# Three one-bank PSUM tiles in place of one three-bank tile at the opening of an expert stage, and a column copied out in three parts

## The chip, the cores and the metric

The kernel runs on one core of one Trainium2 chip. The metric is the time of one execution on the device in microseconds (us). The engines are named as in the profile: PE does the matmuls (PEld its weight loads), DVE, ACT and POOL are the vector, scalar and gpsimd engines, SP issues the DMAs. PSUM is the buffer into which PE writes; it has eight banks of 512 f32 values per partition, and every one of the eight is in use in the stage that is changed.

## The reference

```python
scores = scale * np.matmul(q_pool, k.transpose(0, 1, 3, 2))   # 2 x 8 heads, q pooled by 2
x = softmax(scores) @ v                                        # -> x of 1152 tokens x 512
gate = 1.0 / (1.0 + np.exp(-(x @ w_gate)))                     # first layer, d_ff 1536
x = (gate * (x @ w_val)) @ w_out
logits = x @ w_gate2                                           # expert stage, E = 8
P = np.exp(logits - logits.max())
for _ in range(8):
    P /= P.sum(1, keepdims=True) + 1e-09
    P /= P.sum(0, keepdims=True) + 1e-09
    P *= N / E
for e in range(E):
    out += P[:, e:e + 1] * (np.maximum(x @ w1[e], 0.0) @ w2[e])
```

Three parts follow each other: attention, a gated first layer, and eight experts of 1024 hidden columns whose outputs are weighted by an eight-fold normalised routing matrix. Matmuls are made of two halves of each number (high and low part), three matmuls for one product.

## The kernel before, in words

The last thing the first layer does is its output product, one 128-column block `c` at a time, for `c` = 0 to 3. Each block is 1152 tokens wide and lies in PSUM as three thirds of `TB` = 384 tokens, each third in a bank of its own. For `c` = 3 the PSUM pools of the first layer are closed and the eight banks of the expert stage are laid out: `B0`, `B1`, `X0`, then one tile `psz` of three banks, whose banks are named `Y1`, `y0`, `y1`, then `X1` and `Y0`. The block `c` = 3 is computed in `psz`. The step `x3` (function `take_x3`) copies all three banks to SBUF with one ACT instruction of 1152 columns; the steps `d10` and `d11` read the first third and half of the second on DVE.

From there on the three banks of `psz` do different work. Each expert is computed in two halves; a half-expert is numbered `hx`, 0 to 15, and takes three phases: two first products (`first_product`, matmul lines 903 to 905) and a second product (`second_product`, lines 1318 to 1323 and the plain product on 1353 to 1355). The products follow a seven-product scheme on 2 x 2 blocks: results are added up in the bank pairs `X0 X1`, `Y0 Y1` and `B0 B1`, copied from one pair to another by the ACT steps `go` (`psB<-psX`, `psB<-psY`, `psB<-psz`), and taken out by DVE (`take`, line 1276, tile `acc`). `y0` holds the plain product of the last 128 tokens (128x512, taken by one DVE instruction of 512 columns), and in the first half-experts the gate logits (lines 1455 and 1458) and their transposes (1469); `y1` holds half of the logits and the column sums of the routing (line 1540). In half-experts with an odd `hx` the second product begins in `Y0 Y1`, in even ones in `X0 X1`.

Every instruction of this stage is a `step` with an engine, a due time, durations and the names of the banks that it reads or writes. `arrange` merges the steps into one list with a greedy rule (which engine is free first, given the planner's own durations), and each engine works through its share in that order. `SHIFT` holds offsets of the due times, by step name. The semaphores are not the planner's: the framework sets them from the reads and writes of each tile. They show in the profile as waits. In the profile `psX` is `X0` or `X1`, `psB` is `B0` or `B1`, `psY` is `Y0`, and `psz` stands for `Y1`, `y0` or `y1`, to be told apart by the line and by the columns.

Of the kernel before, what the change touches and what calls it, by code (L numbers as in the profile page):

```python
# [126 lines left out]
def moe_stack_kernel(ctx: ExitStack, tc: tile.TileContext, q, k, v, wg1, wv1, wo1, wg2, w1, w2, out):  # L127
# [789 lines left out]
    with ExitStack() as pb:  # L917
# [48 lines left out]
        for c in range(KD):  # L966
# [10 lines left out]
            if c < KD - 1:  # L977
                ps = ps_b.tile([P, 3, 512], F32, tag="b", name="pso")
            else:
                pbs.close()  # L980
                ps_f = ctx.enter_context(tc.tile_pool(name="ps_f", bufs=1, space=PSUM, reuse_waits="tile"))
                bank = {k: ps_f.tile([P, 512], F32, tag=k, name=f"ps{k[0]}") for k in ("B0", "B1", "X0")}
                ps = ps_f.tile([P, 3, 512], F32, tag="z", name="psz")
                bank.update((k, ps[:, n]) for n, k in enumerate(("Y1", "y0", "y1")))
                bank.update((k, ps_f.tile([P, 512], F32, tag=k, name=f"ps{k[0]}")) for k in ("X1", "Y0"))
            for fc in range(NFF):
                wt = w[:, :, fc * P:(fc + 1) * P]
                for n in range(3):
                    cols = slice(n * TB, (n + 1) * TB)
                    three(  # L990
                        ps[:, n, 0:TB], wt[:, 0], wt[:, 1], gs[fc][:, 0, cols], gs[fc][:, 1, cols],
                        fc == 0, fc == NFF - 1,
                    )
# [394 lines left out]
    def inputs():  # L1388
# [23 lines left out]
        def take_x3():  # L1412
            copy(xt[3].rearrange("p (n w) -> p n w", n=3), ps[:, :, 0:TB])

# [10 lines left out]
        for n, w in ((0, TB), (1, HT - TB)):  # L1425
            step(
                f"d1{n}", "DVE", t - 2, (470, 270)[n], (560, 360)[n],
                lambda n=n, w=w: join(
                    nc.vector, high(2)[:, n * TB:n * TB + w], ps[:, n, 0:w], high(2)[:, n * TB:n * TB + w],
                    ALU.subtract,  # L1430
                ), (), (), [("x", 2)], least=t, ps=("Y1", "y0")[n],
            )
        step("x3", "ACT", t - 2, 1050, 1140, take_x3, (), (), [("x", 3)], least=t, ps="Y1 y0 y1")
        split("b1", xc[1][:, 0], high, 2, t - 1, ["d10", "d11"])
        split("c1", xb[1][:, 0], high, 3, t, ["x3"])
        less("t1", t + 0.5, lambda: low(0), lambda: low(3), lambda: low(2), ["x3", "g0h", "g0l"], 0, 2, 3)
        split("g1", xc[1][:, 1], low, 0, t + 1.5, ["t1"])
        split("h1", xb[1][:, 1], low, 3, t + 2, ["x3"])
# [151 lines left out]
```

## Time and profile before

| | us |
|---|---|
| median of 3 runs | 1276.05 (1274.38 to 1276.24) |
| the profiled execution | 1273.15 |
| span of its trace | 1271.4 |
| PE busy | 1241.3 |
| DVE busy | 1071.4 |
| ACT busy | 780.0 |
| POOL busy | 710.8 |

Busy times are sums over the span. The rest of the profiled execution's time lies outside the span. The first layer's last product ends at about 516 us of the span, the expert stage takes the rest. Half-experts of the even stretch follow each other at 46 us, so a pair of them (one odd, one even) is a period of 92.32 us.

### The profile page before, as it was taken

The numbers are of one execution on the slowest core, as the hardware profiler recorded it, in microseconds if no ns is written. First come the engines' busy times: TensorE is split into PE (matmuls) and PEld (weight loads), VectorE is DVE, ScalarE is ACT, GpSimd is POOL, SyncE is SP. The second block draws the span as 40 slices with busy tenths as digits, with TensorE's granted clock in tenths as the row PEclk, the third lists the DMA queues.
The fourth block names the chain that finished last, engine by engine and source line by source line (L and its number), as shares of the span: only waits on it lengthen the run. The fifth ranks groups of instructions, "written<-read, shape, count | busy, mean of one in ns | idle before, by whom it ended". The sixth has DMA issues, their size and how long they took to land.

```text
span 1271.4 us, 23695 instructions
## 1 busy us (share of the span) xinstructions
PE 1241.3 (98%) x8924; PEld 1206.2 (95%) x8924; DVE 1071.4 (84%) x1954; ACT 780.0 (61%) x1773; POOL 710.8 (56%) x751
## 2 busy tenths in 40 slices
PE   8999999998999999999999999999999999999998
PEld 6889999998999999898999999999999999999998
DVE  7999999997666664888998898898888888888887
ACT  8999999983333322756457557556645645745753
POOL 7778888664434333653564564454555546455552
PEclk9999999999999999999999999999999999999999
DMA  5111220113222331111111111111111111111112
GB/s 163 44 48 56 58 57 13 34 35 99 83 84 85 98 100 51 48 36 34 48 52 36 51 51 34 51 51 51 48 51 37 51 51 34 51 51 51 34 34 76
DMA packets 61204, 70.50 MB, mean 55 GB/s; under 512 B 3360, under 2 KB 47776, under 8 KB 61088
## 3 DMA queue, kind: packets, MB, share of 16 engines
q1 hardware_dynamic: 61088, 68.97, 17.5%
q8 instruction: 70, 1.15, 0.4%
q14 instruction: 46, 0.38, 0.1%
HBM read 66.60 MB, written 2.36 MB: 54 GB/s over the span
## 4 chain that ended last, share of the span: by engine, by line
PE 75%; DVE 15%; ACT 5%; issue 3%; POOL 1%; DMA 1%; SPq 0%; DVEq 0%; ACTq 0%; POOLq 0%
PE psb L905 4%; PE psb L904 4%; PE psb L903 4%; PE psX L903 4%; PE psX L905 4%; PE psX L904 4%; PE psX L1318 3%; PE psX L1323 3%; PE psX L1322 3%; PE psg L542 3%; DVE pT L523 3%; PE psg L503 3%; DVE acc L1276 3%; PE psz L903 2%; PE psz L904 2%
## 5 line engine op out<-in xcount | busy, mean ns | idle before, releaser
L1058 POOL TENSOR_TENSOR sm<-xs 128x512 f32<-128x512 f32 x64 | 92.3, 1452 | 182.2 <-ACT xs L1055 155.4
L1055 ACT ACTIVATE w_two<-sm 128x512 fp32r<-128x512 f32 x128 | 77.8, 629 | 156.5 <-POOL sm L1058 134.8
L1058 POOL TENSOR_TENSOR sm<-raw_w 128x256 f32<-128x256 f32 x128 | 102.9, 824 | 125.5 <-DMA raw_w<-in_moe_w_dram 74.5
L1058 DVE TENSOR_TENSOR hb<-sm,hb 128x512 fp32r<-128x512 f32 x128 | 116.7, 934 | 24.9 <-ACT hb L1055 24.8
L542 PE MATMUL psg<-pT,vs 128*128 128x256 f32 (+1 forms) x576 | 133.0, 318 | 0.1
L1058 DVE TENSOR_TENSOR w_two<-sm,w_two 128x512 fp32r<-128x512 f32 x128 | 112.8, 890 | 5.0 <-ACT w_two L1055 5.0
L1318 PE MATMUL psX<-w_two,hb 128*128 128x256 f32 x384 | 108.7, 283 | 0.2 <-DVE acc L1274 0.2
L523 DVE TENSOR_TENSOR pT<-psg,pT 128x384 fp32r<-128x384 f32 x192 | 102.1, 552 | 7.5 <-ACT pT L519 5.5
L1323 PE MATMUL psX<-w_two,hb 128*128 128x256 f32 x384 | 108.3, 282 | 0.0
L1322 PE MATMUL psX<-w_two,hb 128*128 128x256 f32 x384 | 108.0, 281 | 0.0
L503 PE MATMUL psg<-ident,p 128*128 128x128 f32 x648 | 104.3, 273 | 0.9 <-DVE pT L523 0.3
L1055 ACT ACTIVATE hb<-sm 128x512 fp32r<-128x512 f32 x128 | 75.8, 626 | 45.6 <-POOL sm L1058 44.4
L905 PE MATMUL psb<-x,w_gv 128*128 128x384 f32 x288 | 97.0, 337 | 3.6 <-POOL w_gv L217 3.6
L904 PE MATMUL psb<-x,w_gv 128*128 128x384 f32 x288 | 96.9, 337 | 0.0
L903 PE MATMUL psb<-x,w_gv 128*128 128x384 f32 x288 | 96.9, 336 | 0.0
L542 PEld LDWEIGHTS psg<-pT,vs 128*128 128x128 f32 x576 | 91.2, 189 | 3.5 <-DVE pT L523 0.4
L519 ACT ACTIVATE pT<-psg 128x384 fp32r<-128x384 f32 x192 | 90.3, 497 | 6.0 <-PE psg L503 4.6
L1058 POOL TENSOR_TENSOR sm<-raw_w,sm 128x256 f32<-128x256 f32 x96 | 90.5, 956 | 0.3
L1058 DVE TENSOR_TENSOR w_two<-raw_w,w_two 128x512 fp32r<-128x512 f32 x96 | 75.2, 785 | 17.0 <-ACT w_two L1055 15.3
L1058 DVE TENSOR_TENSOR hb<-xs,hb 128x512 fp32r<-128x512 f32 x96 | 87.5, 924 | 0.0
L503 PEld LDWEIGHTS psg<-ident,p 128*128 128x128 f32 x648 | 78.6, 140 | 6.2 <-issue 1.2
L495 POOL TENSOR_SCALAR p<-p,sum 128x672 f32<-128x672 f32 x72 | 59.6, 828 | 38.5 <-ACT sum L491 34.8
(291 smaller groups left out, 4809.7 us busy)
## 6 DMA issues: line engine op xcount, KB each, us to landing
raw_w<-in_moe_w_dram SPq DMA_DIRECT2D x64, 512.0 KB, 3.5
raw_gv<-in_moe_w_gate_dram SPq DMA_DIRECT2D x12, 512.0 KB, 3.6
raw_gv<-in_moe_w_val_dram SPq DMA_DIRECT2D x12, 512.0 KB, 3.5
raw_o<-in_moe_w_out_dram SPq DMA_DIRECT2D x12, 512.0 KB, 3.5
vr<-in_v_dram SPq DMA_DIRECT2D x16, 288.0 KB, 2.8
kr<-in_k_dram SPq DMA_DIRECT2D x15, 288.0 KB, 2.8
qr<-in_q_dram SPq DMA_DIRECT2D x15, 256.0 KB, 3.4
out_dram<-acc SPq DMA_DIRECT2D x8, 256.0 KB, 2.2
```

The costliest lines, as they stand in the source:

```text
L503: nc.tensor.transpose(have["tpp", i, u, g][:, n * P:(n + 1) * P], have["p", i, u][:, jj * P:(jj + 1) * P], ident)
L519: nc.scalar.activation(out=p_parts(i, u, g)[0], in_=turned(i, u, g), func=AF.Copy)
L523: nc.vector.tensor_tensor(out=lo, in0=turned(i, u, g), in1=f(hi), op=ALU.subtract)
L542: nc.tensor.matmul(have["pv", i, j, n][:, 0:HALF[n][1]], have["vs", i, j][:, jj].rearrange("p a d -> p (a d)"), have["pT", i, j, n][s][:, ...
L903: nc.tensor.matmul(ps, wh, xh, start=first, stop=False, skip_group_check=more)
L904: nc.tensor.matmul(ps, wh, xl, start=False, stop=False, skip_group_check=more)
L905: return nc.tensor.matmul(ps, wl, xh, start=False, stop=last, skip_group_check=more).ins
L1055: nc.scalar.activation(out=out_, in_=in_, func=func)
L1058: eng.tensor_tensor(out=out_, in0=a, in1=b, op=op)
L1318: nc.tensor.matmul(out_, h[:, 0, cols], w[:, 0], start=(begins and kk + m == 0), stop=False, skip_group_check=True,)
L1322: nc.tensor.matmul(out_, h[:, 0, cols], w[:, 1], start=False, stop=False, skip_group_check=True)
L1323: nc.tensor.matmul(out_, h[:, 1, cols], w[:, 0], start=False, stop=(m == 1), skip_group_check=True)
```

## The change

The three-bank tile `psz` goes. `Y1`, `y0` and `y1` become tiles of one bank each, made in the same place among the others, so that each name keeps its bank. The first layer's last column block is computed in the three of them (`thirds`). The one copy `x3` becomes three, `x30` to `x32`, one for each bank, with other durations and due times for the planner and without the offset that `SHIFT` holds for the name `x3`; the steps that read the copied block depend on the parts that they need.

```diff
--- before.py
+++ after.py
@@ -976,19 +976,21 @@
             )
             if c < KD - 1:
                 ps = ps_b.tile([P, 3, 512], F32, tag="b", name="pso")
+                thirds = [ps[:, n, 0:TB] for n in range(3)]
             else:
                 pbs.close()
                 ps_f = ctx.enter_context(tc.tile_pool(name="ps_f", bufs=1, space=PSUM, reuse_waits="tile"))
-                bank = {k: ps_f.tile([P, 512], F32, tag=k, name=f"ps{k[0]}") for k in ("B0", "B1", "X0")}
-                ps = ps_f.tile([P, 3, 512], F32, tag="z", name="psz")
-                bank.update((k, ps[:, n]) for n, k in enumerate(("Y1", "y0", "y1")))
-                bank.update((k, ps_f.tile([P, 512], F32, tag=k, name=f"ps{k[0]}")) for k in ("X1", "Y0"))
+                bank = {
+                    k: ps_f.tile([P, 512], F32, tag=k, name=f"ps{k[0]}")
+                    for k in ("B0", "B1", "X0", "Y1", "y0", "y1", "X1", "Y0")
+                }
+                thirds = [bank[k][:, 0:TB] for k in ("Y1", "y0", "y1")]
             for fc in range(NFF):
                 wt = w[:, :, fc * P:(fc + 1) * P]
                 for n in range(3):
                     cols = slice(n * TB, (n + 1) * TB)
                     three(
-                        ps[:, n, 0:TB], wt[:, 0], wt[:, 1], gs[fc][:, 0, cols], gs[fc][:, 1, cols],
+                        thirds[n], wt[:, 0], wt[:, 1], gs[fc][:, 0, cols], gs[fc][:, 1, cols],
                         fc == 0, fc == NFF - 1,
                     )
             if c < KD - 1:
@@ -1409,9 +1411,6 @@
                 port=630 if eng == "DVE" else 1300,
             )
 
-        def take_x3():
-            copy(xt[3].rearrange("p (n w) -> p n w", n=3), ps[:, :, 0:TB])
-
         t = START
         split("a0", x12[:, 0], low, 0, t - 12, least=t - 12)
         less("d0", t - 14, lambda: high(0), lambda: low(1), lambda: high(0), (), 0, 1)
@@ -1426,16 +1425,21 @@
             step(
                 f"d1{n}", "DVE", t - 2, (470, 270)[n], (560, 360)[n],
                 lambda n=n, w=w: join(
-                    nc.vector, high(2)[:, n * TB:n * TB + w], ps[:, n, 0:w], high(2)[:, n * TB:n * TB + w],
+                    nc.vector, high(2)[:, n * TB:n * TB + w], thirds[n][:, 0:w], high(2)[:, n * TB:n * TB + w],
                     ALU.subtract,
                 ), (), (), [("x", 2)], least=t, ps=("Y1", "y0")[n],
             )
-        step("x3", "ACT", t - 2, 1050, 1140, take_x3, (), (), [("x", 3)], least=t, ps="Y1 y0 y1")
+        for n, k in enumerate(("Y1", "y0", "y1")):
+            step(
+                f"x3{n}", "ACT", t - 2 + 0.1 * n, 400, 490, lambda n=n: copy(xt[3][:, n * TB:(n + 1) * TB], thirds[n]),
+                (), (), [("x", 3)], least=t - 0.5 + 0.25 * n, ps=k,
+            )
+        x3 = [f"x3{n}" for n in range(3)]
         split("b1", xc[1][:, 0], high, 2, t - 1, ["d10", "d11"])
-        split("c1", xb[1][:, 0], high, 3, t, ["x3"])
-        less("t1", t + 0.5, lambda: low(0), lambda: low(3), lambda: low(2), ["x3", "g0h", "g0l"], 0, 2, 3)
+        split("c1", xb[1][:, 0], high, 3, t, x3[1:])
+        less("t1", t + 0.5, lambda: low(0), lambda: low(3), lambda: low(2), [*x3[:2], "g0h", "g0l"], 0, 2, 3)
         split("g1", xc[1][:, 1], low, 0, t + 1.5, ["t1"])
-        split("h1", xb[1][:, 1], low, 3, t + 2, ["x3"])
+        split("h1", xb[1][:, 1], low, 3, t + 2, x3[:2])
         less("f1", t + 2.5, lambda: high(3), lambda: high(3), lambda: high(2), ["c1h", "c1l", "d10", "d11"], 2, 3, eng="POOL")
         split("i1", xd[:, 1], high, 3, t + 4, ["f1"], eng="POOL")
         split("a1", x12[:, 1], low, 2, t + 5, eng="POOL")
```

In the changed kernel the profile's names are `psY` for `Y0` and `Y1` and `psy` for `y0` and `y1`, and line numbers past the change are 2 to 4 higher.

The built order of PE and POOL and that of the DMAs are the same before and after, apart from names. On ACT and DVE about a dozen instructions at the opening of the expert stage change places; after that all orders agree. These are ACT's rows at the opening, before (`xs<-psz 128x1152` is `x3`, `xc` and `xb` are operand splits, `psB<-psX` are the two `go` copies of half-expert 0, `xs<-psY` and `xs<-psz 128x288` a result taken out):

```order
656 L1055 ACTIVATE xs<-psz 128x1152
657 L1055 ACTIVATE xc_5619<-xs 128x576
658 L1055 ACTIVATE xb_4974<-xs 128x576
659 L1055 ACTIVATE psB<-psX 128x288
660 L1055 ACTIVATE xc_5619<-xs 128x576
661 L1055 ACTIVATE psB<-psX 128x288
662 L1055 ACTIVATE xs<-psY 128x288
663 L1055 ACTIVATE xb_4974<-xs 128x576
664 L1055 ACTIVATE xs<-psz 128x288
665 L1055 ACTIVATE w_two<-raw_w 128x512
```

and after:

```order
656 L1057 ACTIVATE xs<-psY 128x384
657 L1057 ACTIVATE xs<-psy 128x384 x2
658 L1057 ACTIVATE xb_4974<-xs 128x576
659 L1057 ACTIVATE xc_5621<-xs 128x576
660 L1057 ACTIVATE xb_4974<-xs 128x576
661 L1057 ACTIVATE psB<-psX 128x288
662 L1057 ACTIVATE xc_5621<-xs 128x576
663 L1057 ACTIVATE xs<-psY 128x288
664 L1057 ACTIVATE psB<-psX 128x288
665 L1057 ACTIVATE w_two<-raw_w 128x512
666 L1057 ACTIVATE xs<-psY 128x288
```

The three copies stand where the one stood. One `xb` split has moved ahead of the first `xc` split, the second `xb` split ahead of the `go` copies, and a result copy (`xs<-psY`) between the two `go` copies.

What else differs is which instructions wait. These are PE's rows in the second product of half-expert 3, at the passage from bank `Y0` to bank `Y1`, with the semaphores that a row waits for, before:

```order
4353 L1322 MATMUL psY<-w_two,hb 128x256
4354 L1323 MATMUL psY<-w_two,hb 128x256
4355 L1318 MATMUL psz<-w_two,hb 128x256 [waits DVE_49]
4356 L1322 MATMUL psz<-w_two,hb 128x256
4357 L1323 MATMUL psz<-w_two,hb 128x256
```

and after:

```order
4357 L1324 MATMUL psY<-w_two,hb 128x256
4358 L1325 MATMUL psY<-w_two,hb 128x256
4359 L1320 MATMUL psY<-w_two,hb 128x256
4360 L1324 MATMUL psY<-w_two,hb 128x256
4361 L1325 MATMUL psY<-w_two,hb 128x256
```

The first matmul into `Y1` waited for DVE and waits for nothing any more. Followed to the instruction that raises the semaphore, the wait of before is one for DVE's take of `y0` (the plain product, 128x512). The same place in the half-experts 5, 7, 9, 11 and 13 reads the same.

On ACT the `go` copy out of `Y1` (`psB<-psz 128x512`) waits for PE in both kernels. Followed in the same way, before it is released by the last matmul of the plain product (into `y0`), after by the last matmul of the first product (into `Y1`). Waits of the same sort, on another bank of `psz`, stand before the change at the first column sums of the routing and at the gate logits, and are waits on the bank itself after it.

## Rows read from the trace of the kernel before

**Rows 1.** The page, part 1: engine, busy us, share of the span, instructions.

```profile
PE 1241.3 (98%) x8924; PEld 1206.2 (95%) x8924; DVE 1071.4 (84%) x1954; ACT 780.0 (61%) x1773; POOL 710.8 (56%) x751
```

**Rows 2.** By stretch (routing, a period): us; PE, PEld, DVE, ACT, POOL busy; clock.

```profile
585.80:638.30 52.50, 49.52 (x371) 47.54 (x370) 49.27 (x106) 28.64 (x63) 27.58 (x25) 1.00 0.13 43
697.85:790.17 92.32, 91.03 (x698) 89.52 (x697) 80.72 (x135) 54.31 (x121) 48.64 (x49) 1.00 0.15 47
```

**Rows 3.** PE's waits over the span: total us, times, longest us.

```profile
PE psz L1318 <- DVE acc L1276: 4.9, 6, 0.8
...
PE psY L1318 <- ACT psB L1055: 2.8, 6, 0.5
```

**Rows 4.** ACT's waits over the span, same columns.

```profile
ACT psB L1055 <- PE psz L1355: 24.8, 7, 3.5
```

**Rows 5.** Timeline, PE, half-expert 3: start, duration, line, tiles, [idle before <-releaser].

```profile
698.59 0.39 PE L1318 MATMUL psY<-w_two,hb 128*128 128x256 f32 x1 [0.47 <-ACT psB L1055]
...
705.65 0.28 PE L1322 MATMUL psY<-w_two,hb 128*128 128x256 f32 x1
705.77 0.28 PE L1323 MATMUL psY<-w_two,hb 128*128 128x256 f32 x1
706.87 0.39 PE L1318 MATMUL psz<-w_two,hb 128*128 128x256 f32 x1 [0.82 <-DVE acc L1276]
```

**Rows 6.** Timeline, DVE, half-expert 3.

```profile
696.44 1.90 DVE L1058 TENSOR_TENSOR hb<-sm,hb 128x512 fp32r<-128x512 f32 x3 [2.10 <-ACT hb L1055]
698.25 1.65 DVE L1276 SCALAR_TENSOR_TENSOR acc<-psX,pr,acc 128x256 f32<-128x256 f32 x4
...
706.08 0.74 DVE L1276 SCALAR_TENSOR_TENSOR acc<-psz,pr,acc 128x512 f32<-128x512 f32 x1
```

**Rows 7.** Timeline, ACT, half-expert 3.

```profile
695.29 0.58 ACT L1055 ACTIVATE psB<-psz 128x512 f32<-128x512 f32 x1 [3.54 <-PE psz L1355]
695.78 1.66 ACT L1055 ACTIVATE hb<-sm 128x512 fp32r<-128x512 f32 x3
...
697.96 0.58 ACT L1055 ACTIVATE psB<-psY 128x512 f32<-128x512 f32 x1
```

**Rows 8.** Timeline, PE, half-expert 3: last matmul of the first product into Y1.

```profile
692.16 0.28 PE L1323 MATMUL psz<-w_two,hb 128*128 128x256 f32 x1
```

**Rows 9.** Timeline, POOL, half-expert 3.

```profile
691.78 1.41 POOL L1058 TENSOR_TENSOR sm<-sm,xs 128x512 f32<-128x512 f32 x1 [0.70 <-DVE w_two L1058]
```

**Rows 10.** Timeline, ACT, opening of the expert stage.

```profile
516.90 1.13 ACT L1055 ACTIVATE xs<-psz 128x1152 f32<-128x1152 f32 x1 [2.36 <-DVE xs L1058]
...
519.62 0.39 ACT L1055 ACTIVATE psB<-psX 128x288 f32<-128x288 f32 x1
```

**Rows 11.** Timeline, DVE, opening of the expert stage.

```profile
518.07 0.36 DVE L1058 TENSOR_TENSOR xs<-psz,xs 128x192 f32<-128x192 f32 x1 [1.20 <-ACT xs L1055]
```

**Rows 12.** Timeline, PE, the waits of the opening, the gate logits and the routing.

```profile
520.07 0.40 PE L903 MATMUL psX<-xc,w_two 128*128 128x288 f32 x1 [0.41 <-ACT psB L1055]
...
530.99 0.30 PE L1455 MATMUL psz<-xa,wgs 128*16 128x288 f32 x1 [0.49 <-ACT xs L1055]
...
532.75 0.31 PE L1455 MATMUL psz<-xa,wgs 128*16 128x288 f32 x1 [0.54 <-ACT xs L1055]
...
535.33 0.40 PE L903 MATMUL psz<-xa,w_two 128*128 128x288 f32 x1 [0.55 <-ACT xs L1055]
...
589.55 0.25 PE L1540 MATMUL psz<-cs,ones 128*128 128x8 f32 x1 [0.56 <-ACT xs L1055]
```

**Rows 13.** Timeline, DVE, routing.

```profile
585.84 0.17 DVE L1497 TENSOR_SCALAR cs<-psz 128x8 f32<-128x8 f32 x1 [1.44 <-PE psz L905]
...
589.12 0.28 DVE L1493 TENSOR_REDUCE cs<-pr 128x8 f32<-128x72 f32 x1
...
592.43 0.46 DVE L1058 TENSOR_TENSOR xs<-psY,xs 128x288 f32<-128x288 f32 x1 [0.33 <-PE psY L905]
```

**Rows 14.** The page, part 5: busy us, mean ns of one, idle before.

```profile
L1058 DVE TENSOR_TENSOR hb<-sm,hb 128x512 fp32r<-128x512 f32 x128 | 116.7, 934 | 24.9 <-ACT hb L1055 24.8
```

## The prediction

> **What bounds the kernel now.** I read the page first: PE is busy 98% of the span, DVE 84% [rows 1]. In the regular part of the expert stage, one period of two half-experts is 92.32 us, of which PE works 91.03, DVE 80.72, ACT 54.31 and POOL 48.64, at full clock [rows 2]. So the time is PE's work plus the little that PE waits, and a change that leaves PE's instructions and their order alone can gain only from those waits. I read them next: apart from the gate logits and the routing, two repeat, six times each and always of the same length. A matmul of the second product into `psz` waits for a DVE take, and one into `psY` for an ACT copy into `psB` [rows 3]. On ACT the longest repeated wait behind a matmul is that of the copy `psB<-psz`, seven times up to 3.5 us, for line 1355, the plain product [rows 4].
>
> Then the timeline at one of the six places, to see what was waited for. PE begins a matmul of 256 columns every 0.12 us though each lasts 0.28 [rows 5]: the next one starts 0.16 before the last ends, so a wait costs its idle time and 0.16 more. PE goes from `Y0` to `Y1` at 705.77 and starts again at 706.87: 1.10 instead of 0.12, that is 0.98 lost. What ended the wait is DVE's `acc<-psz` of 512 columns, 706.08 to 706.82 [rows 6]. That one reads `y0`. PE is about to write `Y1`, another bank, which shares only the name `psz`. The second wait is of the same origin, one step further off. PE's first matmul into `Y0` at 698.59 waits for the `go` copy out of `Y0`, which ACT runs at 697.96, last of a queue that began at 695.29 with the `go` copy out of `Y1`, after 3.54 us of idling for the plain product [rows 7]. But the product in `Y1` that it copies was complete at 692.44 (692.16 and 0.28) [rows 8]. The plain product went into `y0`.
>
> So the trace shows waits on banks that the waiting instruction doesn't touch, and PE pays for two of them in every period.
>
> **The change part by part.** Work: PE, POOL and the DMAs keep all their instructions and their order. ACT has two more, since one copy of 1152 columns (1.13 us) becomes three of 384. None of 384 columns in this place is in the rows; between 0.39 for 288 and 1.13 for 1152 [rows 10] the straight line gives 0.47 each, 1.41 in sum if they don't overlap, 1.13 if the fixed part hides entirely. I take 1.3; it is on no path, as the opening shows.
>
> *The take.* With one tile per bank the wait at 706.87 is gone and nothing stands in its place on that row. Six times 0.98 is 5.9 us. DVE's take of `y0` then runs while PE fills `Y1`. Behind the waiting matmul stood all of PE, so the rest moves up by as much.
>
> *The go copy.* ACT is free at 691.75 (695.29 less 3.54), so the copy out of `Y1` can start when its own bank is ready, at about 692.5 instead of 695.29. Behind it stand three `hb` splits; the first needs POOL's sum that ends at 693.19 [rows 9], so they start at 693.2 instead of 695.78, 2.58 earlier. The `go` copy out of `Y0` follows 2.18 after their start, as it does now (697.96 less 695.78): 695.4 to 696.0. PE wants `Y0` at 697.96 (698.59 less 0.63), 2 us later, so that wait goes whole: 0.47 and 0.16, six times, 3.8 us. Next late on DVE: the `hb` splits it idles for until 696.44 (2.10 for ACT) come about 2 us earlier, so DVE starts its takes at 698.25 earlier as well and isn't left behind by a PE that leads by 1.6 us. If ACT came no earlier, this term would be nothing; that is its lower bound.
>
> *The opening.* ACT's copy at 516.90 waited for DVE's first read [rows 10], and DVE, free at 516.87, waited for ACT until 518.07 [rows 11]. After the change the third pieces can be copied as each bank is finished, and DVE goes on at about 516.9: 1.2 us earlier. The first `go` copy stands 1.55 behind that DVE step now (519.62 less 518.07); in the new order the same two ACT splits' worth of work lies between, so it runs at about 518.4 to 518.8. PE wants the bank at 519.50 (520.07 less 0.57) [rows 12]. The result copy put ahead of the second `go` copy delays that one by another 0.4 at most; PE comes to its bank a product later, which I count as cover. The loss of 0.41 and 0.16 goes: 0.6 us. If the new ACT order were worse than this, the loss would stay or double: bounds of the gain are 0.6 and minus 0.6.
>
> *Gate logits.* Three waits, 0.65, 0.70 and 0.71 with the 0.16 [rows 12]. The third is a first product into `Y1` that waits for ACT's copy out of `y1`; it goes. The first two wait for ACT's copies out of `y0` and `y1`, which are really needed, but each copy waited itself for the matmuls of the other bank and so can start one bank's matmuls earlier, unless ACT is busy. Bounds 0.7 and 2.1; I take 1.7, near the upper end, because ACT works about half the time (28.64 of 52.50 in the routing that follows [rows 2]).
>
> *Routing.* DVE's column step at 585.84 idled 1.44 us for line 905, a matmul into another bank [rows 13]. PE in turn stood until 589.55 [rows 12]; the row names ACT, but DVE's `cs` of the same sums ends at 589.40 [rows 13], so it was DVE. With DVE 1.44 earlier PE's 0.56 and 0.16 go. DVE can't keep more than that: at 592.43 it waits for PE already [rows 13]. And from 585.8 to 638.3 it is busy 49.27 of 52.50 [rows 2], so it sets the pace there and PE's other small waits in that stretch give back what they save. 0.7 us, between 0 and 1.4.
>
> Sum: 5.9 + 3.8 + 0.6 + 1.7 + 0.7 = 12.7 us, from the profiled 1273.15 to 1260.5. The median of the runs lies 2.9 higher, at 1276.05; from there the sum gives 1263.4. I say 1263.5.
>
> Against all of this speaks a rule. Rows 5 show 0.98 us lost at a passage between two banks. The Trainium skill, Perfetto Trace Analysis, section Optimizing Tensor Performance, says that independent groups of matmuls should rotate through different PSUM banks so that taking out one overlaps the matmuls of the next. By that rule this kernel had its overlap already, since it uses the same eight banks in the same turns before and after, and the sum would be 0. The trace disagrees: 0.82 us idle at just such a passage.
>
> **The rivals.** *Only the take's wait goes.* For it: the `go` copy out of `Y0` stands behind five other ACT instructions, and any of them may wait for POOL or DVE (POOL's sum itself waited for DVE, 0.70 [rows 9]). Against it: ACT idles 3.54 ahead of them. Without the 3.8 the gain is 8.9: 1267.2.
>
> *DVE takes the lead back.* PE gains 1.6 us a period, and DVE, busy 80.72 of 92.32, runs late for a take, so that PE waits at the next bank instead. For it: the routing stretch, where DVE does set the pace. Against it: 11.6 us of DVE idling per period, 2.10 of it in the very place. If all regular gains went, 0.6 + 1.7 + 0.7 would be left: 1273.0, on the edge of what can be told.
>
> *Same banks, no change.* The rule above as a mechanism: bank rotation already gives the overlap, and what ends the waits is needed in any case. It gives 1276. The forms in rows 5 and 6 (512 columns read, 256 written) speak against it.
>
> *Slower.* POOL's sums follow DVE's `hb` splits, and would move 2 us up with them, onto DVE's own splits. These take 0.63 each in the run of three at 696.44, but 0.93 in the mean [rows 14], so some of them are held up already. If two POOL sums of 1.41 [rows 9] came to lie on DVE work wholly, DVE would lose 2.8 us in each period and PE with it, if it had no slack. It ends on the slower side once it costs more than 2.1 us a period (12.7 over six). At 2.8 the time is 1276.05 + 6 x 2.8 - 12.7, 1280.
>
> **How the numbers follow.** About 0.2% (2.5 us) is what a measurement of this kernel tells from no change. Both waits go: 0.58. Only the take's: 0.22. DVE takes the lead back: 0.10, half of it on the faster side of that bound. No change: 0.05. Slower: 0.05. Faster then has 0.58 + 0.22 + 0.05 = 0.85, the same 0.05 + 0.05 = 0.10, slower 0.05. The range takes in the first two cases: down to 1260.5 (the upper bounds of logits and routing, 0.4 and 0.7 more, and the spread of the runs shown, 1.9), up to 1270.5 (the second case with the logits, opening and routing at their lower ends, 2.3 less and a little more).
>
> **What would show it.** Right: PE's waits no longer list DVE `acc` and ACT `psB` six times, ACT's wait of 3.5 us for the plain product is gone, and a period measures about 90.7 us instead of 92.32. At the opening three ACT copies of 128x384 begin near 515, 515.5 and 516.0, and the matmul at 520.07 comes without a wait. The expert stage reaches the period at 697.85 some 3 us earlier. Wrong: a period that stays above 91.3 means the `go` copy is still late; one of 92.3 with a new PE wait at DVE's `acc` or `hb` means DVE took the lead back; DVE splits whose mean rises above 0.93 mean POOL lies on them.

## The result, and the profile after the change

The changed kernel takes 1259.88 us in the median of 4 runs (1258.98 to 1260.56); the kernel before, run beside it, 1275.22 (4 runs). The ratio is 0.9881, 95% interval [0.9864, 0.9898]: 15 us faster. The forecast was 1263.5, with a range that begins at 1260.5, 0.6 above the result. Between the two profiled executions the forecast sum was 12.7 us (1273.15 to 1260.5), and the profiled execution of the changed kernel took 1260.09. The mechanism held; what missed is the step from a profiled execution to the median, which half of the runs below are about, and the price of a stall, which was 0.10 too low.

The page of the changed kernel, part 1, beside [rows 1]: PE's busy time falls by 3.5 us, that of DVE and POOL rises by 2.4 and 5.0.

```profile
PE 1237.8 (98%) x8924; PEld 1205.8 (96%) x8924; DVE 1073.8 (85%) x1954; ACT 780.3 (62%) x1775; POOL 715.8 (57%) x751
```

The two stretches of [rows 2], taken between the same matmuls. A period is 90.50 us instead of 92.32, and PE works in all of it: nothing is left to gain there but PE's own work.

```profile
583.38:635.51 52.13, 49.98 (x371) 47.62 (x370) 49.05 (x105) 28.51 (x63) 27.49 (x25) 1.00 0.16 50
695.06:785.56 90.50, 90.50 (x698) 89.40 (x697) 81.50 (x134) 54.30 (x120) 49.66 (x49) 1.00 0.15 48
```

PE's waits after the change, same columns as [rows 3]. Both repeated waits are gone. One in the routing stays, and one at 893.55 is new and comes once.

```profile
PE psy L1544 <- DVE cs L1497: 1.0, 1, 1.0
...
PE psY L903 <- DVE acc L1278: 0.4, 1, 0.4
```

PE's timeline at the two places, half-expert 3. The matmul that began at 698.59 after 0.47 of idling is the one at 695.17 here, 0.11 after its predecessor; the one at 706.87 after 0.82 [rows 5] is the one at 702.37, also 0.11.

```profile
695.06 0.28 PE L1325 MATMUL psX<-w_two,hb 128*128 128x256 f32 x1
695.17 0.28 PE L1320 MATMUL psY<-w_two,hb 128*128 128x256 f32 x1
...
702.26 0.28 PE L1325 MATMUL psY<-w_two,hb 128*128 128x256 f32 x1
702.37 0.28 PE L1320 MATMUL psY<-w_two,hb 128*128 128x256 f32 x1
702.50 0.28 PE L1324 MATMUL psY<-w_two,hb 128*128 128x256 f32 x1
```

ACT there. The clocks of the two profiles differ by 2.79 us at this point (697.85 less 695.06). Put on the clock of before, the `go` copy out of `Y1` runs at 692.48 (forecast 692.5, before 695.29 [rows 7]), the three splits at 693.22 (forecast 693.2), the `go` copy out of `Y0` at 695.41 (forecast 695.4 to 696.0, before 697.96); it starts 2.55 ahead of PE's matmul.

```profile
689.69 0.58 ACT L1057 ACTIVATE psB<-psY 128x512 f32<-128x512 f32 x1 [0.74 <-PE psY L1325]
690.43 1.67 ACT L1057 ACTIVATE hb<-sm 128x512 fp32r<-128x512 f32 x3 [0.15 <-POOL sm L1060]
...
692.62 0.57 ACT L1057 ACTIVATE psB<-psY 128x512 f32<-128x512 f32 x1
```

The opening on ACT, where one copy ran at 516.90 [rows 10]: three copies from 515.57 on, 1.50 us in sum (forecast 1.3), and the first `go` copy at 518.89 (518.33 on the clock of before, 0.56 less; forecast 518.4 to 518.8).

```profile
515.57 0.49 ACT L1057 ACTIVATE xs<-psY 128x384 f32<-128x384 f32 x1 [0.48 <-PE psY L905]
516.09 1.01 ACT L1057 ACTIVATE xs<-psy 128x384 f32<-128x384 f32 x2
...
518.89 0.39 ACT L1057 ACTIVATE psB<-psX 128x288 f32<-128x288 f32 x1
```

PE passes the opening without a wait (0.13 after the matmul at 519.93; before 0.70 after that at 519.37), reaches the gate logits' three places [rows 12] at 530.28, 531.34 and 533.19, and ends on the matmul at 1253.18.

```profile
519.93 0.30 PE L905 MATMUL psY<-xa,w_two 128*128 128x288 f32 x1
520.06 0.29 PE L903 MATMUL psX<-xc,w_two 128*128 128x288 f32 x1
...
530.28 0.31 PE L1459 MATMUL psy<-xa,wgs 128*16 128x288 f32 x1
...
598.69 0.39 PE L1544 MATMUL psy<-cs,ones 128*128 128x8 f32 x2 [1.05 <-DVE cs L1497]
...
1253.18 0.27 PE L1325 MATMUL psY<-w_two,hb 128*128 128x256 f32 x1
```

**A ladder of start times.** Both kernels issue the same 8924 matmuls in the same order, so the start of each can be subtracted from that of its counterpart, and a wait that goes shows as a step. I use one number throughout: the *expert stretch*, from the last matmul ahead of the opening's wait, in half-expert 0's first product, to the last matmul of all. These are its ends before the change; the length is 746.89. After the change it is 1253.18 less 519.93, 733.25: 13.6 us shorter. The spans differ by 13.1, since the changed kernel's profile reached the start of the stretch 0.56 later.

```profile
519.37 0.29 PE L905 MATMUL psz<-xa,w_two 128*128 128x288 f32 x1
...
1266.25 0.28 PE L1323 MATMUL psz<-w_two,hb 128*128 128x256 f32 x1
```

| step of the ladder, us | forecast | found |
|---|---|---|
| opening | 0.6 | 0.78 |
| gate logits | 1.7 | 2.03 |
| routing | 0.7 | 0.55 |
| take's wait, 6 times | 5.9 | 6.5 (1.08 each) |
| `go` copy's wait, 6 times | 3.8 | 4.4 (0.73 each) |
| the new wait at 893.55 and small ones | 0 | -0.6 |
| sum | 12.7 | 13.6 |

### The profile page after: what moved, and what is told of

Read it like the earlier page. It is cut to its first block, busy times and chain, and to the rows that moved or that the text cites. A ratio compares the mean times of both kernels' runs of the same rounds, so it can differ in the third digit from the quotient of the medians.

```text
span 1258.3 us, 23700 instructions
## 1 busy us (share of the span) xinstructions
PE 1237.8 (98%) x8924; PEld 1205.8 (96%) x8924; DVE 1073.8 (85%) x1954; ACT 780.3 (62%) x1775; POOL 715.8 (57%) x751
## 4 chain that ended last, share of the span: by engine, by line
PE 79%; DVE 12%; ACT 4%; POOL 2%; issue 2%; DMA 1%; SPq 0%; DVEq 0%; ACTq 0%; POOLq 0%
PE psb L905 4%; PE psb L904 4%; PE psb L903 4%; PE psY L903 4%; PE psY L904 4%; PE psY L905 4%; PE psX L903 4%; PE psX L904 3%; PE psX L905 3%; PE psX L1320 3%; PE psX L1325 3%; PE psX L1324 3%; PE psY L1320 3%; PE psY L1325 3%; PE psY L1324 3%; PE psg L542 3%
## 5 line engine op out<-in xcount | busy, mean ns | idle before, releaser
L1060 DVE TENSOR_TENSOR hb<-sm,hb 128x512 fp32r<-128x512 f32 x128 | 119.5, 961 | 9.0 <-ACT hb L1057 9.0
L1320 PE MATMUL psY<-w_two,hb 128*128 128x256 f32 x384 | 108.5, 283 | 0.0
L1324 PE MATMUL psY<-w_two,hb 128*128 128x256 f32 x384 | 108.2, 282 | 0.0
L1325 PE MATMUL psY<-w_two,hb 128*128 128x256 f32 x384 | 108.0, 281 | 0.0
L1060 POOL TENSOR_TENSOR sm<-raw_w,sm 128x256 f32<-128x256 f32 x96 | 93.1, 983 | 0.3
```

The lines of the kernel that those rows point to most:

```text
L1060: eng.tensor_tensor(out=out_, in0=a, in1=b, op=op)
L1320: nc.tensor.matmul(out_, h[:, 0, cols], w[:, 0], start=(begins and kk + m == 0), stop=False, skip_group_check=True,)
L1324: nc.tensor.matmul(out_, h[:, 0, cols], w[:, 1], start=False, stop=False, skip_group_check=True)
L1325: nc.tensor.matmul(out_, h[:, 1, cols], w[:, 0], start=False, stop=(m == 1), skip_group_check=True)
```

## The experiments

The theory: with three banks in one tile an instruction waits for work on a neighbour's bank, and PE pays for that at the places of the table. The rivals: the copy in three parts and ACT's new order bring the gain; it is the number or size of tiles that counts, not which banks share; and, for the excess of the medians over the ladder, something in the expert stage that before's one profile didn't show. The diffs below are cut to the lines that matter.

| kernel | expert stretch, us | median, us (runs) |
|---|---|---|
| before_low_last | 748.0 | 1275.57 (11) |
| before, five profiles | 746.9 to 747.5 | 1274.7 (46) |
| copies_alone | 747.2 | 1274.71 (11) |
| before_no_row_eps | 745.6 | 1272.27 (11) |
| Y1_y0_one_tile | 743.7 | 1270.02 (6) |
| go_wait_back | 738.4 | 1266.80 (5) |
| y0_y1_one_tile | 733.8 | 1261.96 (4) |
| tiles_alone | 733.3 | 1261.32 (4) |
| after, two profiles | 733.2, 733.3 | 1259.6 (8) |
| after_low_last | 732.6 | 1260.39 (4) |
| routing_wait_back | 732.6 | 1260.30 (4) |
| after_no_row_eps | 731.6 | 1257.85 (4) |

**copies_alone.** After the change, with the three banks again in one tile (`one` makes a tile of one bank for each name).

```diff
-    for k in ("B0", "B1", "X0", "Y1", "y0", "y1", "X1", "Y0")
+    one("B0", "B1", "X0")
+    pz = ps_f.tile([P, 3, 512], F32, tag="z", name="psz")
+    bank.update((k, pz[:, n]) for n, k in enumerate(("Y1", "y0", "y1")))
+    one("X1", "Y0")
```

> The copy in three parts and the order it brings, with the one three-bank tile kept. Theory (the waits on a neighbour's bank are the whole of it): both regular waits of PE stay, six times about 0.8 us on DVE's take and six times about 0.5 on the go copy, ACT's 3.5 us in front of the plain product stays, and the gate logits keep their three waits; only the opening may move, by at most 0.6 us either way. So 1274.6 to 1275.8 beside a kernel before at 1275.2, a ratio of 0.9995 to 1.0005. Rival (the gain comes from the new order of ACT's work): the regular waits shrink, at least half of the 15 us is there, 1267 or less.

Measured: 1274.71, ratio 0.9998 [0.9989, 1.0006]. PE's waits are those of [rows 3] to the tenth:

```profile
PE psz L1322 <- DVE acc L1280: 4.9, 6, 0.8
...
PE psY L1322 <- ACT psB L1059: 2.8, 6, 0.5
```

The order of ACT's work brings nothing while the tile is shared.

**tiles_alone.** Three tiles, and the column copied out in one step at its old place.

```diff
-            step(f"x3{n}", "ACT", t - 2 + 0.1 * n, 400, 490, lambda n=n: copy(xt[3][:, n * TB:(n + 1) * TB], thirds[n]),
+    def take_x3():
+        for n in range(3):
+            copy(xt[3][:, n * TB:(n + 1) * TB], thirds[n])
+    step("x3", "ACT", t - 2, 1050, 1140, take_x3, (), (), [("x", 3)], least=t, ps="Y1 y0 y1")
```

> Three tiles of one bank, with the last column copied out in one step at the old place (three instructions in a row), so that every engine has the order of before. Theory: the regular waits go (12 stalls, 10 us by the trace after the change), the gate logits give 1.4 to 2.1 and the routing 0.6; the opening keeps its 0.41 us wait. The span is 12 to 13 us below that of before, the ratio 0.989 to 0.991. Rival (the order of the three copies is needed for the go copy to come early): the go waits stay, the gain is below 9 us, ratio 0.993 or more.

Measured: 1261.32, ratio 0.9894 [0.9879, 0.9909], expert stretch 733.31, as after the change. All twelve stalls are gone, and so is the new wait at 893.55. What the three separate steps add is seen at the opening alone. There DVE again waits for ACT (0.94, before 1.20 [rows 11]), the `go` copy is late for PE as before, and PE loses 0.31 to the matmul at 521.18 (0.44 behind that at 520.74, where 0.13 is usual; the idle time in it is 0.15, where 0.41 was expected) and 0.10 at each of two matmuls behind it:

```profile
519.18 0.36 DVE L1060 TENSOR_TENSOR xs<-psy,xs 128x192 f32<-128x192 f32 x1 [0.94 <-ACT xs L1057]
```

So the tiles are nearly all of the change; by the ladder the copy in parts is worth 0.5 us at the opening and 0.1 at each of two later places (531.72 and 758.90). The medians differ by more, 1.7; the profile of tiles_alone reached the expert stretch 0.8 later.

**Which banks share.** Two kernels with a tile of two banks and one bank apart; the rest as after the change.

```diff
+    pz = ps_f.tile([P, 2, 512], F32, tag="z", name="psz")
+    bank.update((k, pz[:, n]) for n, k in enumerate(("y0", "y1")))    # y0_y1_one_tile
+    bank.update((k, pz[:, n]) for n, k in enumerate(("Y1", "y0")))    # Y1_y0_one_tile
```

> After the change, but y0 and y1 share one tile of two banks; Y1 has its own. Theory: the pair Y1 and y0 alone makes the regular waits (the take reads y0 while PE wants Y1; the go copy reads Y1 while the plain product is written to y0), so both are gone: 10 us. Of the gate logits the wait for Y1 goes (0.7) and the two on y0 and y1 stay (1.4 lost again). The gain is 11 to 12 us of the 13 of the traces: 1 to 2 us above the changed kernel, ratio to before 0.9895 to 0.9915. Rival (it is the size of the shared tile or the number of tiles, not which banks share): about half of the regular waits come back, 1265 or more.

> After the change, but Y1 and y0 share one tile of two banks; y1 has its own. Theory: all twelve regular stalls are back with their lengths of before (0.8 on the take and 0.5 on the go copy), and only the gate logits (0.7 to 2.1), the routing (0.6) and the opening (0 to 0.6) are gained: 2 to 3 us, 1272 to 1273.5 beside 1275.2, ratio 0.9975 to 0.9985. Rival (size of the tile, not which banks share): as the kernel with y0 and y1 in one tile, within 1 us.

Measured: with `y0` and `y1` together 1261.96, ratio 0.9901 [0.9886, 0.9917]; with `Y1` and `y0` together 1270.02, 0.9965 [0.9952, 0.9977]. PE's waits with `y0` and `y1` together show no regular one, but the routing's and two of the logits':

```profile
PE psz L1546 <- DVE acc L1278: 1.7, 1, 1.7
...
PE psz L1461 <- ACT xs L1059: 1.0, 2, 0.5
```

With `Y1` and `y0` together both regular ones are back in full, the logits' are gone and the routing's is 1.1:

```profile
PE psz L1322 <- DVE acc L1280: 4.9, 6, 0.8
...
PE psY L1322 <- ACT psB L1059: 2.8, 6, 0.5
```

The tiles have the same size and number in both; 9.8 us of expert stretch hang on the pair. (The first kernel's stretch is only 0.6 longer than that of the changed one, because the wait at 893.55 doesn't come in it. The second kernel's stretch is 3.2 shorter than that of before, near the 2 to 3 expected; its median falls by more, 4.9, and lies below the 1272 to 1273.5 expected, of which below.) So the rule that the forecast weighed isn't enough here (the Trainium skill, Perfetto Trace Analysis, Optimizing Tensor Performance: rotate through the banks). Both kernels rotate through the same eight banks in the same turns, and one of them waits twice in every period. The Trainium skill's PSUM — Partial Sum Buffer, section PSUM bank collisions raise a hardware error, says to guard PSUM with semaphores by bank and quadrant, or more simply by bank. The runs agree so far as time goes: guarding by a tile of three banks cost 13.6 us of expert stretch here, by one of two banks 10.4 or 0.6, according to the pair.

**go_wait_back.** After the change, with one wait put back by hand and nothing else moved on any engine: in the odd half-experts the `go` copy out of `Y1` waits for the last matmul of the plain product.

```diff
+    ended[0] = nc.tensor.matmul(py, h[:, 1], w[:, 0], start=False, stop=(x == 3)).ins
+    i = nc.scalar.activation(out=bank[f"B{n}"], in_=bank[f"{a}{n}"], func=AF.Copy).ins
+    if n == 1 and hx % 2 and ended[0] is not None:
+        tc.add_manual_dep(
+            i, ended[0].name, mybir.DependencyInfo(mybir.DependencyClass.Sync, mybir.DependencyReason.DATA),
+            reason="plain",
+        )
```

> After the change, with one wait put back by hand in the odd half-experts: the go copy out of Y1 waits for the end of the plain product (which writes another bank), as it did before. Theory: ACT's queue is late again by that much, the go copy out of Y0 is late for PE six times, and PE loses 0.47 idle and about 0.26 around it each time: 4.4 us above the changed kernel, in steps of 0.73; the take's wait doesn't come back. Rival (the go copy has slack, and what made it late was the order or the take's wait): no step at that place, within 1 us of the changed kernel.

Measured: 1266.80, ratio 0.9936 [0.9924, 0.9949], 7 us above the changed kernel. ACT's rows are those of before again, wait and all, and so is PE's:

```profile
694.54 0.58 ACT L1363 ACTIVATE psB<-psY 128x512 f32<-128x512 f32 x1 [3.54 <-PE psy L1359]
695.03 1.66 ACT L1057 ACTIVATE hb<-sm 128x512 fp32r<-128x512 f32 x3
...
697.21 0.58 ACT L1363 ACTIVATE psB<-psY 128x512 f32<-128x512 f32 x1
```

```profile
697.85 0.39 PE L1320 MATMUL psY<-w_two,hb 128*128 128x256 f32 x1 [0.47 <-ACT psB L1363]
...
1172.86 0.40 PE L903 MATMUL psX<-xc,w_two 128*128 128x288 f32 x1 [0.65 <-ACT psB L1057]
```

The ladder against the changed kernel has six steps of 0.73, 4.4 in sum, as expected; the take's wait stays away. The expert stretch is 5.1 longer in all: two more waits come, at 1172.86, where ACT is late once more (0.9), and at 1079.90 (0.3), and the wait at 893.55 doesn't come (0.67). So the chain from the plain product through ACT's queue to PE is shown by itself. The two profiled executions are 7.15 apart, since this one reached the expert stretch 2.0 us later than that of the changed kernel; why such distances arise is what the next runs are about.

**Why the medians differ by more than the ladder.** In the profiles of before and after PE waits 3.6 us for the first weights of the gate, near 290 us, and soon after runs at 1.2 GHz instead of 2.4 for a while (a granted clock of 0.83 over 290:300): its matmuls of 384 columns then follow each other by 0.32 us instead of 0.17. Runs differ in their mean granted clock, and the time follows it. Of the 46 runs of before, those at 0.998 take 1273.7 in the mean, at 0.997 1274.8, at 0.996 1276.2. The first guess was that this wait makes the scatter. Two kernels change the order of the first gate product: those matmuls first that don't need the low part of the weights (`s` is the half of the weights, `part` that of `x`).

```diff
+    if fc == 0:
+        for s, part in ((0, 0), (0, 1), (1, 0)):
+            for c in range(KD):
+                for n in range(3):
+                    nc.tensor.matmul(ps[:, n, 0:TB], wr[:, s, i, c], x1[c][:, part, n * TB:(n + 1) * TB],
+                                     start=(c + s + part == 0), stop=(s == 1 and c == KD - 1))
```

> The kernel before, with the first gate product's matmuls in another order (all that need only the high parts of the weights first, those with the low part last), so that PE has 24 matmuls to do while POOL makes the low part at 289 to 290 us. Theory on the scatter: the 3.6 us wait and the half-clock stretch behind it go, 5 to 7 us less than before in the median, the mean granted clock is 1.00 in every run, and the runs lie within 1.5 us of each other instead of 3.5. Rival (the scatter and the offset between a profiled run and the median come from elsewhere): 3.6 us less at most, and runs still scattered over 3 us.

> The changed kernel with the same new order in the first gate product. Theory: as before_low_last, 5 to 7 us below the changed kernel (1253 to 1255), and, with the scatter gone from both, the difference between the medians of before_low_last and this one is what the ladder of start times gives for the expert stage, 13.6 us (13.3 to 13.9), not the 15 us between the medians of before and after. Rival: the difference stays at 15 us or more, so that something in the expert stage costs before 1.5 us that its profile doesn't show.

Measured: 1275.57 (11 runs), ratio 1.0007 [0.9998, 1.0016], and 1260.39 (4 runs), 0.9891 [0.9876, 0.9906]. The expectation failed: nothing is gained, because the wait only changed its name. PE now waits as long for POOL's last piece of `x`, which is finished at 291.35:

```profile
PE psb L937 <- POOL x L168: 3.7, 1, 3.7
```

The second expectation failed too, on the side of its rival: the two medians differ by 15.2, not by 13.3 to 13.9. So do the expert stretches of the two profiles, 748.0 and 732.6, by 15.4. The shorter one has the expert stage of the changed kernel without the wait at 893.55 (0.64).

The longer one shows something else, a stretch at half clock in the expert stage, behind PE's 1.6 us wait of the routing. The matmuls take 0.41 and follow each other by 0.21 instead of 0.12, for 3.4 us:

```profile
602.02 0.39 PE L1548 MATMUL psz<-cs,ones 128*128 128x8 f32 x2 [1.61 <-DVE acc L1282]
...
603.31 0.41 PE L1330 MATMUL psX<-w_two,hb 128*128 128x256 f32 x1
603.53 0.41 PE L1331 MATMUL psX<-w_two,hb 128*128 128x256 f32 x1
...
606.48 0.28 PE L1330 MATMUL psX<-w_two,hb 128*128 128x256 f32 x1
```

The change shortens this wait to 1.05, so a new theory arose: before's runs have this stretch often, and its first profile is one without it.

**after_again**, the changed kernel once more, gives 1259.32 (4 runs, 1258.93 to 1262.63), ratio 0.9885 [0.9871, 0.9900], and an expert stretch of 733.18: the same within 0.1.

> The changed kernel once more, to size its gain and its scatter better. Theory: the time of a run follows the half-clock stretch behind PE's 3.6 us wait at 290 us, which differs from run to run; by the ladder of PE's start times the expert stage alone is 13.6 us shorter, so the median stands 13 to 15 us below that of before, and the profile shows the same expert stage within 0.2 us. Rival (something in the expert stage differs from run to run and made before's median 2 to 3 us worse than its profile): the expert stage of this second profile differs from the first by 1 us or more.

**routing_wait_back** puts that one wait back into the changed kernel: the seventh column sum waits for DVE's take of `y0` too.

```diff
+    m = nc.tensor.matmul(bank["y1"][:, 0:E], ones, small["cs"][:, 0], start=True, stop=True).ins
+    if i == 6:
+        tc.add_manual_dep(
+            m, taken[NT - 1].name, mybir.DependencyInfo(mybir.DependencyClass.Sync, mybir.DependencyReason.DATA),
+            reason="take",
+        )
```

> After the change, with one single wait of before put back by hand: the routing's seventh column sum on PE (into y1) also waits for DVE's take of y0. In the trace PE's wait there grows from 1.05 to about 1.65 us and DVE, which sets the pace there, gives nearly all of it back by 608 us, so the trace alone says 0 to 0.6 us more. Theory on why before's median lies 1.4 to 2.9 us above its profiled run: a PE wait of 1.6 us at this place brings a half-clock stretch of about 3 us in some executions, as the profile of before_low_last shows at 603 to 606 us, and a wait of 1.05 doesn't. Then the median rises by 1 to 2 us, to 1260.6 to 1261.6, and the mean granted clocks fall towards 0.997. Rival (that stretch is chance and has nothing to do with the length of this wait): within 0.6 us of the changed kernel's 1259.6.

Measured: 1260.30 (4 runs), ratio 0.9888 [0.9874, 0.9901]. The wait is back (1.67 instead of 1.05), the ladder shows a step of 0.52 that is given back by 607 us (the expert stretch is even 0.7 shorter, since the wait at 893.55 doesn't come), and no half-clock stretch follows:

```profile
600.69 0.39 PE L1510 MATMUL psy<-cs,ones 128*128 128x8 f32 x2 [1.67 <-DVE acc L1278]
```

The median lies between the two expectations, so it decides nothing; the trace speaks for the rival.

**before_no_row_eps and after_no_row_eps** leave out the addition of 1e-9 to the row sums, eight DVE instructions ahead of the column sums. The expectation took 1.3 us for each; in the traces only three take that, the other five 0.17 to 0.45.

```diff
-        nc.vector.tensor_scalar(out=rs, in0=rs, scalar1=1e-9, scalar2=None, op0=ALU.add)
```

> The kernel before, without the addition of 1e-9 to the row sums in the eight rounds of the routing (that part of the computation is left out). It takes 1.3 us of DVE each time, ahead of the column sums that PE waits for. Theory (the half-clock stretch at the routing follows the 1.6 us wait): the wait falls to 0.3 to 0.7 us, 1.5 to 3 us are gained in the trace, and the median comes to lie within 1 us of the profiled run, 3 to 5 us below before's 1274.7, with mean clocks of 0.998 and more. Rival (DVE is held up by POOL at that place and the next instruction pays instead): no gain, 0 to 0.5 us, and the clocks stay at 0.997.

> The changed kernel, without the addition of 1e-9 to the row sums in the eight rounds of the routing (that part is left out). Theory: what is left of PE's waits in the routing (0.3, 1.05, 0.2, 0.5 us) mostly goes, 1 to 2.5 us below the changed kernel's 1259.6. The DVE bound of that stretch is then seen: it gains at most what DVE is relieved of, 8 x 1.3 less what other work waits for. Rival (the hold-up moves to the next DVE instruction): within 0.5 us.

Measured: 1272.27 (11 runs), ratio 0.9987 [0.9976, 0.9998], and 1257.85 (4 runs), 0.9868 [0.9853, 0.9883]. In before the wait falls to 1.1, not to 0.3 to 0.7, and the runs scatter as before (1270.2 to 1276.2); the expert stretch is 1.3 shorter, which neither expectation had. In the changed kernel it is 1.7 shorter, within the 1 to 2.5 expected, 0.5 of it by the wait at 893.55 that doesn't come. The addition took 1.29 and its neighbours 0.2; with it gone the next instruction but one takes 1.10, where after the change it took 0.23. First the changed kernel's rows, then those without the addition, each with POOL's row beside them:

```profile
596.49 1.29 POOL L1060 TENSOR_TENSOR sm<-sm,xs 128x512 f32<-128x512 f32 x1 [1.30 <-DVE rs L1493]
596.52 1.29 DVE L1494 TENSOR_SCALAR rs<-rs 128x9 f32<-128x9 f32 x1
...
598.09 0.23 DVE L1496 TENSOR_TENSOR pr<-pr,rs 128x72 f32<-128x72 f32 x1
```

```profile
595.57 1.29 POOL L1060 TENSOR_TENSOR sm<-sm,xs 128x512 f32<-128x512 f32 x1 [1.30 <-DVE rs L1493]
...
595.34 0.22 DVE L1493 TENSOR_REDUCE rs<-pr 128x9 f32<-128x72 f32 x1
595.60 0.21 DVE L1494 RECIPROCAL rs<-rs 128x9 f32<-128x9 f32 x1
595.84 1.10 DVE L1495 TENSOR_TENSOR pr<-pr,rs 128x72 f32<-128x72 f32 x1
```

A hold-up of about 0.9 us moves on, as the rival said. The traces show beside what it comes: in both pairs of kernels the three instructions of 1.1 to 1.3 us run beside a POOL sum of 128x512 that takes 1.28 to 1.30, and end 0.03 to 0.10 behind it; the three additions with no POOL work beside them take 0.17. No run takes POOL's sum away, so that it is the cause isn't shown. The second of these kernels is 1.7 us below the changed one, the lowest time of this study, with that part of the computation missing.

**Four more profiles of before** were to show where its executions differ.

> The kernel before, one more profile (one of four). Its median over 46 runs, 1274.7, lies 1.6 us above its first profile. Theory A (the half-clock stretch at 603 to 606 us behind the 1.6 us wait comes in most executions and makes that offset, and the change shortens the wait): at least two of the four profiles show it, each 1.4 us. Theory B (the offset is made ahead of the expert stage, in the length of the half-clock stretch at 290 us and now and then at 10 to 20 us, and the first profile was an execution with little of it): at most one of four shows a stretch at the routing, and the start times at 520 us differ by 1 to 3 us between the profiles, as the run times do.

> The second of the four profiles of the kernel before; the expectation is that of the first.

 

> The third of the four profiles of the kernel before; the expectation is that of the first.

 

> The fourth of the four profiles of the kernel before; the expectation is that of the first.

They took 1273.69, 1273.91, 1276.24 and 1275.91. None has a half-clock stretch in the expert stage, and their expert stretches are 747.4, 747.5, 746.9 and 746.9. The two longer executions lose all of their 3 us ahead of it: 1.8 in the first 20 us, the rest (1.2 and 0.8) around the wait at 290. Two stretches of the third by the granted clock (the column before the last two), which is 1.00 in 10:20 and 0.83 in 290:300 in the first profile of before:

```profile
10.00:20.00 10.00, 8.21 (x49) 7.10 (x48) 7.20 (x12) 7.03 (x20) 8.96 (x11) 0.83 0.63 177
290.00:300.00 10.00, 8.31 (x32) 8.31 (x33) 8.30 (x14) 3.60 (x5) 5.58 (x5) 0.66 0.46 142
```

The two shorter ones lose 0.5 to 0.6 within it, by a wait for a take that the first profile hasn't:

```profile
1086.27 0.40 PE L903 MATMUL psz<-xa,w_two 128*128 128x288 f32 x1 [0.31 <-DVE acc L1276]
```

By its expectation that speaks for theory B: the 3 us between executions of before arise in attention and at its end, for the most part by stretches of half clock that differ from execution to execution. At equal granted clock the kernels differ by less than by their medians: at 0.998, 1273.7 (13 runs) against 1259.4 (4 runs), 14.3 us. The ladder's 13.6 lies inside both intervals measured for the change (13.0 to 17.3 and 12.7 to 16.4 us).

Open is the last us or so between them. For chance speak four other kernels: tiles_alone, y0_y1_one_tile, routing_wait_back and after_low_last gain 13.6, 13.0, 14.6 and 14.1 us in the median, each beside its own runs of before, and 13.6, 13.0, 14.3 and 14.3 by the ladder. On the other side stand short waits that come in some executions only. The wait at 893.55 is in both profiles of the changed kernel and in none of the others; without it the ladder has 14.3, and 14.9 against a profile of before with the wait at 1086. And there is the half-clock stretch of before_low_last. These runs can't tell which of them the unprofiled executions have.

## Why the prediction was right, and where it was wrong

- *What bounds the kernel.* Right: the gain came from PE's waits alone, PE's order being the same.
- *The take.* Right in kind, 6.5 instead of 5.9. The price "idle and 0.16" is 0.10 too low, in all twelve stalls: behind a wait not only the waiting matmul is late, the one after it comes 0.22 later instead of 0.12. In the trace of before this row follows the one at 706.87 [rows 5]:

```profile
707.09 0.28 PE L1322 MATMUL psz<-w_two,hb 128*128 128x256 f32 x1
```

- *The go copy.* Right, link by link, and shown alone by go_wait_back; 4.4 instead of 3.8 for the same 0.10.
- *The opening.* 0.78 for 0.6, near the instants that were forecast. Of it 0.5 comes from the copy in parts, the rest from the tiles. The three copies take 1.50, above the upper bound of 1.41 worked out for them, on no path.
- *Gate logits.* 2.03 for 1.7, near the upper bound of 2.1.
- *Routing.* 0.55 for 0.7. DVE sets the pace there, as was said: the step of 0.55 at 602 was given back within 6 us.
- *Where DVE could fall behind.* PE meets one new wait for a take, at 893.55, which costs 0.67; none was forecast for the sum. The sign named for POOL on DVE's splits did appear: their mean rose from 934 ns [rows 14] to 961, and POOL's busy time by 5 us. DVE's slack took it up.

```profile
L1060 DVE TENSOR_TENSOR hb<-sm,hb 128x512 fp32r<-128x512 f32 x128 | 119.5, 961 | 9.0 <-ACT hb L1057 9.0
```

- *The step that failed:* "The median of the runs lies 2.9 higher, at 1276.05; from there the sum gives 1263.4." It took the distance between one profiled execution and a median of three runs for a constant that the changed kernel would have too. The runs show that it belongs to the execution: over 46 runs before's median lies 1.6 above that profile, not 2.9, its third and fourth extra profiles lie 3 above the first, and the changed kernel's first profile lies 0.5 above its median over 8 runs, not 2.9 below. How much of this the change itself makes is the open us above.
- *The term that was too small:* the price of a stall. Twelve times 0.10 were missing, and the range left no room for them: its lower end adds something for the logits, the routing and the scatter of the runs, nothing for the two regular waits. That the sum came out within 0.5 us from profile to profile (1260.5 and 1260.09) is in part luck: the ladder found 13.6 where the sum has 12.7, and 0.56 of it was lost ahead of the stretch.
- *The rivals.* Only the take's wait: refuted, both went. DVE takes the lead back: 0.67 once, not in every period. Same banks, no change: refuted by Y1_y0_one_tile and y0_y1_one_tile. Slower through POOL: the sign came, at no price. (At the upper end of the range the lower bounds of logits, opening and routing, as they were given, are 2.9 less, not 2.3; the end named, 1270.5, still holds that.)

## What to carry to other kernels

Where banks of one PSUM tile go through different hands, give each its own tile: the waits that a shared name makes don't show as waits on that bank, but as a releaser that touches another one, and they reach PE through a queue (here ACT's) as well as directly. Price a stall by the start times around it, up to the second matmul behind it. And forecast from profile to profile: the distance of one execution to the median isn't carried along, unless it is known where in the program it is made.

## What the runs showed of the hardware that was not expected

- A matmul behind a wait takes 0.39 us instead of 0.28, and its successor starts 0.22 later instead of 0.12 (706.87, 697.85 in go_wait_back): 0.10 us in each of the twelve stalls, and in the six put back by hand.
- Half clock comes at some waits of PE and not at others of the same length: in one profile behind the 1.6 us wait of the routing (1.4 us lost), in none of eight others with that wait at 1.6 or 1.7; at the wait of 3.6 us near 290 in every profile, for a time that differs (0.83 and 0.66 of the clock in 290:300 in the first profile of before and the third extra one).
- A small DVE instruction in the routing takes 1.1 to 1.3 us where its neighbours take 0.2, each time beside a POOL sum of 1.28 to 1.30 us and ending 0.03 to 0.10 behind it. Which instruction pays isn't fixed: with the addition taken out, another one did. That POOL's sum is the cause wasn't tried.
